# Zero-padded v of the last keys made by GpSimd, preparation at 1.2 items a tile, three splits of nine on VectorE, and three units of weights put together beside attention pairs 3, 6 and 9

## The chip, the cores and the metric

The kernel runs on one core of one Trainium2 chip. The metric is the device time of one execution in microseconds, given as the median of several runs. The engines are named as in the profile: PE is TensorE, PEld its weight loads, DVE is VectorE, ACT is ScalarE, POOL is GpSimd, SP is SyncE, on whose queue all transfers are issued.

## The reference

Three layers in a row, all in float32; the six weight matrices come as float64.

```python
def _attn_ref(q, k, v, tau):                # (4, 8, 576, 64) each
    scores = 1/np.sqrt(64) * np.matmul(q, k.transpose(0, 1, 3, 2))
    thresh = np.max(scores, axis=-1, keepdims=True) - tau
    scores = np.where(scores >= thresh, scores, -1000000000.0)
    scores = scores - np.max(scores, axis=-1, keepdims=True)
    attn = np.exp(scores)
    attn = attn / (np.sum(attn, axis=-1, keepdims=True) + 1e-09)
    return np.matmul(attn, v)
...
x = attn_out.transpose(0, 2, 1, 3).reshape(2304, 512)
g = x @ w_gate                              # (512, 1536)
x = (g / (1 + np.exp(-g)) * (x @ w_val)) @ w_out
return ((x @ w1) * (x @ w2) @ w3) @ w_out2  # d_ff 1024
```

## The kernel before

Every product of large matrices is made of float32r parts: a number is kept as hi plus lo, and hi·hi, hi·lo and lo·hi are added up in PSUM (`mm3`, L835). So every operand must be split into hi and lo first, and much of what the other engines do is such splitting.

**Pairs and tiles.** The attention works on 16 pairs of heads, four to each of the four batches, counted from 0. A pair has nine tiles: four of 128 queries for each of its two heads, and tile 4, which holds the last 64 queries of both. For a tile PE makes the scores into one of two banks S (`mm_scores`, L443); DVE takes the row maximum and brings the scores to SBUF (`el_max`, L482); ACT makes the exponentials (`el_exp`, L491); POOL makes the threshold (`el_thr`, L474); DVE masks and sums (`el_mask`, L501), three tiles behind.

**Two queues of items.** Behind a pair's tile 4 and tile 8 its other work goes into the queue `main`: transposes of the masked tiles through one of four banks T (`it_T`, `it_lq`, `it_kl`, `it_corner`; L328), and the products with v (`it_pv`, L583 and L588). The queue `prep` holds the preparation of the next pair: `it_k`, `it_q` (transposes, hi), `it_k2`, `it_q2` (lo, and transfers that stack hi and lo into L and R) and `it_left` (the last 64 tokens). `it_k` and `it_q` hold a bank T each until `it_k2` and `it_q2` have read it. `some(frac)` runs items by credit: 19.5/9 items of `main` and 0.8 of `prep` a tile. At tile 7 what is left of `prep` is run at once. The instructions written so are then ordered on each engine by a scheduler when the program is built.

**Paths of a split.** The transposed tiles are split out of their bank T by `evac_split` in one of three ways, in the order of the string PATHS: Z: ACT copies hi, PE subtracts it in the bank (L335), ACT copies lo. X: ACT copies hi, DVE subtracts from the bank into lo (L524). Y: ACT copies the bank to SBUF (L535), POOL makes hi (L100) and lo (L103). Before, nine splits in a row are Y Z X Z Y Z X Z Y: three of Y, four of Z, two of X; one copy of path Y in seven goes into a tile of its own, `raw`. In the last pair X and Z take turns.

**v of the last 64 keys.** For the product L588 the v of one head's last 64 keys stands in a tile VLZ of 128 partitions whose other half is zero. `split_left(b)` splits the last v of a batch on POOL into `vls`, once a batch, and `split_v(p)` moves its pair's two parts into VLZ with two transfers on SP (L309).

**Units of weights.** A unit is 128 x 512 numbers of a weight matrix, turned from float64 to hi and lo. `conv_step` starts one unit and ends the one started before: DVE L139, L142, L145, ACT L148, L149, POOL L150 (`conv_bits`), and later DVE L157, ACT L196, and L199 on POOL or DVE by turns. A unit needs a slot of 4 KB a partition. Three slots exist from the start (N_U1), seven more when the last pair begins (N_U2), eight more when its end is near (N_U3).

**The last pair.** When pair 15 begins, `early()` puts seven items into `prep`: three `conv_step` and four `x_prep(0, kk)`, which load the first block of x (the attention's output, through DRAM), add its two halves (POOL L826), multiply by the reciprocal sums (DVE L829) and split it (ACT L817, DVE L818) into four slots; each load takes two slots and gives them back after L829. `begin()` then mixes the first products of the second layer (`glu_step`, L835) with the attention's last items. Every `glu_step` needs its three units put together (`conv_until`).

Of the kernel before, what the change touches and what calls it, by code (L numbers as in the profile page):

```python
# [9 lines left out]
F32 = mybir.dt.float32  # L10
F32R = mybir.dt.float32r
# [12 lines left out]
N_U1, N_U2, N_U3, N_U4 = 3, 7, 8, 24  # L24
N_TMP, N_BIG, N_HB, N_TA = 6, 3, 3, 1

GROUP = 2

PATHS, LAST = "YZXZYZXZY", "XZ"
# [3 lines left out]
def kernel(  # L35
# [171 lines left out]

    def conv_step(n=1):

        old = []  # L210
        while conv_mid and conv_mid[0][2]() and len(old) < n:
            old.append(conv_mid.popleft())
            old[-1][1](conv_value(old[-1][0]))
        new = 0
        while (conv_in or conv_raw) and len(conv_mid) < n:
            conv_fetch()
            raw, *rest = conv_raw.popleft()
            conv_mid.append((conv_bits(raw), *rest))
            new += 1
        conv_fetch()  # L220
        return old or new
# [6 lines left out]
    def attention(actx, early, tail):  # L228
# [8 lines left out]
        ta = lctx.enter_context(tc.tile_pool(name="ta", bufs=N_TA))  # L237
        raw_i, in_tail = [0], []

        def raw_tile():  # L240
            raw_i[0] += 1
            if in_tail or raw_i[0] % (N_TA + N_TMP) >= N_TA:
                return tmp()
            return ta.tile([P, 512], F32, tag="raw", name="raw")

# [7 lines left out]
        VLZ = at.tile([P, 2, 2, 2, D], F32R, name="VLZ")  # L253
        nc.gpsimd.memset(f32(VLZ), 0.0)

# [29 lines left out]
        def split_left(b):  # L285
# [11 lines left out]
            vls = wk.tile([P, HP, 2, D], F32R, tag="vls", name="vls", bufs=2)  # L297
            split_pool(vls[:, :, 0, :], vls[:, :, 1, :], vl)
            lsplit[b] = (qks, vls)

        def split_v(p):
# [4 lines left out]
            vls = lsplit[p // HP][1]  # L306
            for h in range(2):
                r = slice(64 * h, 64 * h + 64)
                nc.sync.dma_start(out=f32(VLZ[r, p % 2, h]), in_=f32(vls[r, p % HP]))  # L309
# [100 lines left out]
        def it_left(p):  # L410
            b, hp = divmod(p, HP)
            L, R = qk_tiles(p)
            qks = lsplit[b][0]
# [96 lines left out]
        def evac_split(hi, lo, bank):  # L510
# [17 lines left out]
            else:  # L528
                raw = raw_tile()
# [43 lines left out]
        def it_pv(p, h, n):  # L573
# [13 lines left out]
            for e in range(2):  # L587
                nc.tensor.matmul(  # L588
                    o, lhsT=VLZ[:, p % 2, h, :, :].rearrange("p a d -> p (a d)"),
# [107 lines left out]
        def some(frac):  # L697
            credit[0] += 19.5 / 9 * frac
            credit[1] += (1.5 if in_tail else 0.8) * frac
# [9 lines left out]
        for n, (p, i) in enumerate(tiles):  # L709
# [25 lines left out]
            if n == NS // 2:  # L735
                conv_fetch()
# [218 lines left out]
    def early():  # L955
        add_slots(ctx.enter_context(tc.tile_pool(name="u2", bufs=1, reuse_waits="tile")), N_U2)
        r = [conv_step] * 3
        for kk in range(KD):
            r.insert(2 * kk + 1, lambda kk=kk: x_prep(0, kk))
        return r  # L960
# [172 lines left out]
```

## Time and profile before

| | |
|---|---|
| median of 3 runs | 1187.19 us (1186.79 to 1188.41) |
| the profiled execution | 1189.26 us, its span 1187.3 us |
| PE busy | 1122.1 us, 95% |
| DVE busy | 733.1 us, 62% |
| ACT busy | 590.3 us, 50% |
| POOL busy | 475.7 us, 40% |
| granted TensorE clock, mean | 0.991 |

The span is the time from the first to the last instruction of the profiled execution; some 2 us lie around it. The attention takes the first 360 us, the second layer ends near 815 us, w3 times w_out2 is made from there to 895 us, and the third layer follows. A busy share over the whole span averages over these stages, so the rows below are taken from single stretches. The clock is given as a share of 2.4 GHz; its two levels are 1.2 and 2.4 GHz.

### The profile page before, as it was taken

What the parts mean: (1) busy time and instruction counts of PE and PEld (TensorE: products, weight loads), DVE (VectorE), ACT (ScalarE), POOL (GpSimd) and SP (SyncE); (2) the same over time, 40 slices, a digit from 0 to 9 for tenths busy, and PEclk for the clock granted to TensorE, in tenths of its full rate; (3) what the DMA queues carried; (4) which work ended last, traced back from release to release, by engine and by line L of the source; (5) the groups of instructions that cost most, each with busy time, mean ns of one, the idle gap of its engine ahead of it and who ended that gap; (6) DMA issues with size and microseconds to landing.
All of it is one profiled execution on the core that took longest, in us unless ns stands there. A gap on an engine that the chain in (4) does not pass through costs nothing.

```text
span 1187.3 us, 16882 instructions
## 1 busy us (share of the span) xinstructions
PE 1122.1 (95%) x6074; PEld 959.8 (81%) x6074; DVE 733.1 (62%) x1272; ACT 590.3 (50%) x1071; POOL 475.7 (40%) x457
## 2 busy tenths in 40 slices
PE   7898998899878999999999999999899999999998
PEld 6788888788766777888888888888787888888886
DVE  7987868778798797656464664567892022432222
ACT  6877878778786456443242432345563231321111
POOL 4575665565663655443232332234241221321110
PEclk9999999999989999999999999999999999999999
DMA  8865756656455743222111120123430010100024
GB/s 197 224 146 141 163 132 142 146 121 142 107 170 167 216 126 100 75 68 71 31 59 36 37 89 8 47 93 103 124 107 18 1 36 1 37 1 1 1 58 102
DMA packets 107891, 108.14 MB, mean 91 GB/s; under 512 B 48800, under 2 KB 82208, under 8 KB 107808
## 3 DMA queue, kind: packets, MB, share of 16 engines
q1 hardware_dynamic: 107808, 107.06, 34.3%
q8 instruction: 48, 0.79, 0.3%
q14 instruction: 35, 0.29, 0.1%
HBM read 68.16 MB, written 14.23 MB: 69 GB/s over the span
## 4 chain that ended last, share of the span: by engine, by line
PE 55%; DVE 5%; DMA 2%; ACT 1%; issue 1%; POOL 0%; POOLq 0%; DVEq 0%; ACTq 0%
PE t_bank L835 36%; PE s_bank L835 19%; DMA raw<-in_moe_w_dram 2%; DVE tmp L157 1%; DVE slot L818 1%; DVE raw L142 1%; DVE tmp L145 1%; DVE tmp L139 0%; DVE slot L911 0%; PE t_bank L908 0%; DVE slot L199 0%; DVE slot L1022 0%; DVE slot L882 0%; DVE slot L1059 0%; ACT raw L148 0%
## 5 line engine op out<-in xcount | busy, mean ns | idle before, releaser
L835 PE MATMUL t_bank<-slot,slot 128*128 128x512 f32 (+1 forms) x2592 | 559.7, 371 | 5.9 <-DVE slot L818 2.4
L835 PEld LDWEIGHTS t_bank<-slot,slot 128*128 128x128 f32 x2592 | 457.0, 189 | 92.8 <-DVE slot L818 3.3
L835 PE MATMUL s_bank<-h,slot 128*128 128x512 f32 (+1 forms) x720 | 161.9, 372 | 3.4 <-ACT slot L884 2.2
L150 POOL TENSOR_TENSOR raw<-raw 128x512 int32<-128x512 int32 x76 | 84.4, 1111 | 182.1 <-ACT raw L149 171.6
L501 DVE SCALAR_TENSOR_TENSOR P<-P,stat,E 128x576 f32<-128x576 f32 x144 | 148.3, 1043 | 5.6 <-POOL stat L474 3.9
L835 PEld LDWEIGHTS s_bank<-h,slot 128*128 128x128 f32 x720 | 126.8, 190 | 27.1 <-ACT slot L884 2.6
L482 DVE TENSOR_SCALAR_CACHE_REDUCE P<-s_bank,neg 128x576 f32<-128x576 f32 x144 | 114.2, 809 | 55.2 <-PE s_bank L443 55.2
L1069 DVE TENSOR_TENSOR tmp<-tmp,t_bank 128x512 f32<-128x512 f32 (+1 forms) x40 | 25.3, 633 | 178.2 <-PE t_bank L835 178.2
L107 POOL TENSOR_TENSOR h<-tmp,h 128x512 fp32r<-128x512 f32 (+1 forms) x60 | 74.4, 1239 | 136.1 <-ACT h L106 136.0
L1073 POOL TENSOR_TENSOR h<-tmp,h 128x512 fp32r<-128x512 f32 (+1 forms) x38 | 45.8, 1205 | 200.5 <-ACT h L1071 200.5
L491 ACT ACTIVATE E<-P,stat 128x576 f32<-128x576 f32 x144 | 116.4, 812 | 9.7 <-DVE P L482 8.8
L443 PE MATMUL s_bank<-R,L 128*128 128x288 f32 x512 | 101.2, 318 | 14.7 <-DVE P L482 5.6
L920 DVE TENSOR_TENSOR tmp<-tmp,t_bank 128x512 f32<-128x512 f32 (+1 forms) x60 | 37.9, 631 | 113.1 <-PE t_bank L835 104.5
L835 PE MATMUL s_bank<-slot,h 128*128 128x512 f32 x432 | 106.6, 391 | 0.9 <-DVE slot L1059 0.8
L328 PE MATMUL t_bank<-ident,P 128*128 128x128 f32 x640 | 90.5, 277 | 14.5 <-DVE AT L524 4.7
L443 PEld LDWEIGHTS s_bank<-R,L 128*128 128x128 f32 x512 | 76.8, 194 | 26.7 <-DVE P L482 15.1
L835 PEld LDWEIGHTS s_bank<-slot,h 128*128 128x128 f32 x432 | 79.9, 188 | 18.3 <-DVE slot L1059 2.1
L882 DVE TENSOR_TENSOR slot<-s_bank,slot 128x1024 f32<-128x1024 f32 (+1 forms) x72 | 82.2, 1146 | 18.5 <-PE s_bank L835 16.5
L328 PEld LDWEIGHTS t_bank<-ident,P 128*128 128x128 f32 x640 | 74.2, 141 | 23.5 <-DVE ATL L524 4.6
L583 PE MATMUL t_bank<-AT,sp 128*128 128x288 f32 x512 | 87.5, 307 | 5.3 <-DVE AT L524 2.4
L157 DVE SCALAR_TENSOR_TENSOR tmp<-tmp,raw 128x512 f32<-128x512 f32 x76 | 72.0, 948 | 30.5 <-POOL raw L150 30.5
L919 ACT ACTIVATE tmp<-t_bank 128x512 f32<-128x512 f32 (+1 forms) x60 | 33.2, 554 | 113.3 <-PE t_bank L835 106.9
(110 smaller groups left out, 1427.9 us busy)
## 6 DMA issues: line engine op xcount, KB each, us to landing
raw<-in_moe_w_dram SPq DMA_DIRECT2D x32, 512.0 KB, 3.8
raw<-in_moe_w_out_dram SPq DMA_DIRECT2D x20, 512.0 KB, 3.5
x_dram<-xs SPq DMA_DIRECT2D x64, 144.0 KB, 2.4
L<-qhi SPq DMA_DIRECT2D x60, 128.0 KB, 2.9
L<-qlo SPq DMA_DIRECT2D x60, 128.0 KB, 2.5
raw<-in_moe_w_gate_dram SPq DMA_DIRECT2D x12, 512.0 KB, 3.7
raw<-in_moe_w_val_dram SPq DMA_DIRECT2D x12, 512.0 KB, 3.8
ld<-in_k_dram SPq DMA_DIRECT2D x16, 256.0 KB, 4.0
```

The costliest lines, as they stand in the source:

```text
L107: nc.gpsimd.tensor_tensor(out=lo, in0=src, in1=f32(hi), op=ALU.subtract)
L150: nc.gpsimd.tensor_tensor(out=a, in0=a, in1=x, op=ALU.subtract)
L157: nc.vector.scalar_tensor_tensor(out=f32(m), in0=f32(m), scalar=2.0 ** 20, in1=f32(a), op0=ALU.add, op1=ALU.mult)
L328: nc.tensor.matmul(bank[:, t * P:(t + 1) * P], lhsT=part, rhs=ident, is_transpose=True, start=(t == 0), stop=(t == len(parts) - 1),)
L443: nc.tensor.matmul(o, lhsT=lhs, rhs=R[:, c:c + HALF], start=(h == hs2[0] and e == 0), stop=(h == hs2[-1] and e == 1),)
L482: nc.vector.tensor_scalar(out=p_tile(p, i).rearrange("p (a c) -> p a c", a=2), in0=sb[:, :, 0:HALF], scalar1=neg, scalar2=None, op0=ALU.mu ...
L491: nc.scalar.activation(out=e, in_=p_tile(p, i), func=ACTF.Exp, scale=-1.0, bias=stats[p // HP][:, 0, c:c + 1],)
L501: nc.vector.scalar_tensor_tensor(out=t, in0=t, scalar=stats[b][:, 1, c:c + 1], in1=e, op0=ALU.is_le, op1=ALU.mult, accum_out=sums[b][:, c: ...
L583: nc.tensor.matmul(o, lhsT=vs[:, 4 * h + c, :, :].rearrange("p a d -> p (a d)"), rhs=AT[h][:, e, c, cs], start=(c == 0 and e == 0), stop=F ...
L835: nc.tensor.matmul(o, lhsT=lhs(a), rhs=rhs(c), start=(first and i == 0), stop=(last and i == 2))
L882: nc.vector.tensor_tensor(out=a, in0=s, in1=a, op=ALU.add)
L1073: (nc.vector if end else nc.gpsimd).tensor_tensor(out=h[:, 1, 0:n], in0=ab[:, 0:n], in1=f32(h[:, 0, 0:n]), op=ALU.subtract)
```

## The change

- VLZ becomes two tiles, one for the even and one for the odd batches, each with all four pairs of a batch. `split_left` splits v right into them, a head's half of the partitions at a time: four POOL operations a batch instead of two, and no `vls` and no transfers.
- `prep` runs 1.2 items a tile instead of 0.8.
- PATHS becomes X Z Y X Z Z Y X Z: three of X, four of Z, two of Y. The extra tile for `raw` goes.
- At tile 4 of pairs 3, 6 and 9 a `conv_step` and a new `conv_end`, which ends a started unit, are put into `prep`. `early()` then holds the four `x_prep` alone.
- Slots: six instead of seven when the last pair begins, nine instead of eight later.

The diff, without its two hunks that only take `ta` and `raw_tile` out:

```diff
-N_U1, N_U2, N_U3, N_U4 = 3, 7, 8, 24
+N_U1, N_U2, N_U3, N_U4 = 3, 6, 9, 24
+EARLY = (3, 6, 9)
-PATHS, LAST = "YZXZYZXZY", "XZ"
+PATHS, LAST = "XZYXZZYXZ", "XZ"
...
+    def conv_end(n=1):
+        old = 0
+        while conv_mid and conv_mid[0][2]() and old < n:
+            bits, done, _ = conv_mid.popleft()
+            done(conv_value(bits))
+            old += 1
+        return old
...
-        VLZ = at.tile([P, 2, 2, 2, D], F32R, name="VLZ")
-        nc.gpsimd.memset(f32(VLZ), 0.0)
+        VLZ = [at.tile([P, HP, 2, 2, D], F32R, name=f"VLZ{n}") for n in range(2)]
+        for t in VLZ:
+            nc.gpsimd.memset(f32(t), 0.0)
...
-            vls = wk.tile([P, HP, 2, D], F32R, tag="vls", name="vls", bufs=2)
-            split_pool(vls[:, :, 0, :], vls[:, :, 1, :], vl)
-            lsplit[b] = (qks, vls)
+            for h in range(2):
+                r = slice(64 * h, 64 * h + 64)
+                split_pool(VLZ[b % 2][r, :, h, 0, :], VLZ[b % 2][r, :, h, 1, :], vl[r])
+            lsplit[b] = qks
...
-            vls = lsplit[p // HP][1]
-            for h in range(2):
-                r = slice(64 * h, 64 * h + 64)
-                nc.sync.dma_start(out=f32(VLZ[r, p % 2, h]), in_=f32(vls[r, p % HP]))
...
-                    o, lhsT=VLZ[:, p % 2, h, :, :].rearrange("p a d -> p (a d)"),
+                    o, lhsT=VLZ[b % 2][:, hp, h, :, :].rearrange("p a d -> p (a d)"),
...
-            credit[1] += (1.5 if in_tail else 0.8) * frac
+            credit[1] += (1.5 if in_tail else 1.2) * frac
...
-            if n == NS // 2:
-                conv_fetch()
+            if i == 4 and p in EARLY:
+                prep.extend([conv_step, conv_end])
...
     def early():
         add_slots(ctx.enter_context(tc.tile_pool(name="u2", bufs=1, reuse_waits="tile")), N_U2)
-        r = [conv_step] * 3
-        for kk in range(KD):
-            r.insert(2 * kk + 1, lambda kk=kk: x_prep(0, kk))
-        return r
+        conv_fetch()
+        return x_items(0)
```

The scheduler makes more of it than these lines tell. The rows below are its order of one engine's instructions; the lines of the changed kernel are numbered some three lower (L479, L498 and L521 are the maximum, the mask and the split of path X; L141 to L159 the steps of a unit on DVE, two higher; L826 and L815 the multiplication and split of x). Over the whole program the counts change so: POOL's two operations of path Y 48 to 32 each, DVE's split of path X 40 to 56, transfers 32 fewer; the numbers of PE's and ACT's instructions stay.

DVE early in the last pair, pair 15 (its P tiles are P_4485 to P_4489), before:

```order
L139 TENSOR_SCALAR tmp<-raw 128x512 x3
L482 TENSOR_SCALAR P_4487,stat<-s_bank,neg 128x576
L142 TENSOR_SCALAR raw<-raw 128x512
L145 SCALAR_TENSOR_TENSOR tmp<-raw,tmp 128x512
L482 TENSOR_SCALAR P_4488,stat<-s_bank,neg 128x576
L829 TENSOR_TENSOR tmp<-tmp,slot_4543 128x512
L142 TENSOR_SCALAR raw<-raw 128x512
L145 SCALAR_TENSOR_TENSOR tmp<-raw,tmp 128x512
L501 SCALAR_TENSOR_TENSOR P_4485,sums<-P_4485,stat,E 128x576
L142 TENSOR_SCALAR raw<-raw 128x512
L145 SCALAR_TENSOR_TENSOR tmp<-raw,tmp 128x512
```

and after (P_4467 to P_4471):

```order
L498 SCALAR_TENSOR_TENSOR P_4468,sums<-P_4468,stat,E 128x576
L479 TENSOR_SCALAR P_4469,stat<-s_bank,neg 128x576
L479 TENSOR_SCALAR P_4470,stat<-s_bank,neg 128x576
L498 SCALAR_TENSOR_TENSOR P_4469,sums<-P_4469,stat,E 128x576
L479 TENSOR_SCALAR P_4471,stat<-s_bank,neg 128x576
L498 SCALAR_TENSOR_TENSOR P_4470,sums<-P_4470,stat,E 128x576
L479 TENSOR_SCALAR P_4467,stat<-s_bank,neg 128x576
L826 TENSOR_TENSOR tmp<-tmp,slot_4502 128x512
L521 TENSOR_TENSOR AT<-t_bank,AT 128x512
L479 TENSOR_SCALAR P_4468,stat<-s_bank,neg 128x576
L498 SCALAR_TENSOR_TENSOR P_4471,sums<-P_4471,stat,E 128x576
```

The steps of the units, L139 to L145 here and L157 and L199 further on, are gone from between the pair's maxima and masks.

DVE at the turn from pair 3 to pair 4, where the reciprocal of the sums of the first batch (`r`) is made, before:

```order
L606 TENSOR_SCALAR r<-sums 128x36
L609 RECIPROCAL r<-r 128x36
L482 TENSOR_SCALAR P_1260,stat<-s_bank,neg 128x576
L482 TENSOR_SCALAR P_1261,stat<-s_bank,neg 128x576
L482 TENSOR_SCALAR P_1262,stat<-s_bank,neg 128x576
L501 SCALAR_TENSOR_TENSOR P_1260,sums<-P_1260,stat,E 128x576
L524 TENSOR_TENSOR AT<-t_bank,AT 128x512
L482 TENSOR_SCALAR P_1263,stat<-s_bank,neg 128x576
```

and after:

```order
L141 TENSOR_SCALAR tmp<-raw 128x512
L603 TENSOR_SCALAR r<-sums 128x36
L144 TENSOR_SCALAR raw<-raw 128x512
L147 SCALAR_TENSOR_TENSOR tmp<-raw,tmp 128x512
L606 RECIPROCAL r<-r 128x36
L479 TENSOR_SCALAR P_1264,stat<-s_bank,neg 128x576
L479 TENSOR_SCALAR P_1265,stat<-s_bank,neg 128x576
L159 SCALAR_TENSOR_TENSOR tmp<-tmp,raw 128x512
L498 SCALAR_TENSOR_TENSOR P_1264,sums<-P_1264,stat,E 128x576
L498 SCALAR_TENSOR_TENSOR P_1265,sums<-P_1265,stat,E 128x576
```

The whole of a unit now stands here among the maxima and masks, but for L201, which POOL has for this one.

PE in the preparation of a later pair (`ld` are k and q as loaded, `khi` and `qhi` their hi parts), before:

```order
L328 MATMUL t_bank<-ident,ld_1570 128x128 x4
L335 MATMUL t_bank<-AT,minus_r 128x512
L328 MATMUL t_bank<-ident,P_1549 128x128
L328 MATMUL t_bank<-ident,P_1550 128x128
L328 MATMUL t_bank<-ident,P_1551 128x128
L328 MATMUL t_bank<-ident,P_1552 128x128
L443 MATMUL s_bank<-R,LZ 128x288 x8
L563 MATMUL t_bank<-ident,P_1553 128x128
L564 MATMUL t_bank<-ident,P_1553 64x128
L443 MATMUL s_bank<-R,L 128x288 x4
L335 MATMUL t_bank<-khi,minus_r 128x512
L328 MATMUL t_bank<-ident,ld_1572 128x128 x4
```

and after:

```order
L325 MATMUL t_bank<-ident,ld_1573 128x128 x4
L325 MATMUL t_bank<-ident,ld_1575 128x128 x4
L440 MATMUL s_bank<-R,LZ 128x288 x8
L440 MATMUL s_bank<-R,L 128x288 x4
L325 MATMUL t_bank<-ident,P_1549 128x128
L325 MATMUL t_bank<-ident,P_1550 128x128
L325 MATMUL t_bank<-ident,P_1551 128x128
L325 MATMUL t_bank<-ident,P_1552 128x128
L332 MATMUL t_bank<-AT,minus_r 128x512
L332 MATMUL t_bank<-khi,minus_r 128x512
L332 MATMUL t_bank<-qhi,minus_r 128x512
```

The transposes of k and q have moved next to each other, and so have the subtractions that free their banks.

## Rows read from the trace of the kernel before

**Rows 1.** The page of the profile, part 1 (busy us, share of the span, instructions).

```profile
PE 1122.1 (95%) x6074; PEld 959.8 (81%) x6074; DVE 733.1 (62%) x1272; ACT 590.3 (50%) x1071; POOL 475.7 (40%) x457
```

**Rows 2.** Stretches: start:end, length, busy PE, PEld, DVE, ACT, POOL (instructions), clock, DMA, GB/s.

```profile
26.50:328.60 302.10, 272.26 (x1954) 247.64 (x1953) 246.20 (x562) 244.67 (x496) 181.69 (x206) 0.99 0.63 147
328.60:359.30 30.70, 22.37 (x138) 19.31 (x137) 30.70 (x56) 25.42 (x47) 19.82 (x16) 0.89 0.60 179
...
475.00:815.00 340.00, 340.00 (x1681) 288.75 (x1680) 194.84 (x264) 124.88 (x203) 113.99 (x97) 1.00 0.19 58
```

**Rows 3.** Waits of PE in pair 15 (us in total, times, longest).

```profile
PE t_bank L328 <- DVE ATL L524: 3.3, 1, 3.3
```

**Rows 4.** DVE's groups of the units in pair 15: xcount | busy us, mean ns | idle.

```profile
L157 DVE SCALAR_TENSOR_TENSOR tmp<-tmp,raw 128x512 f32<-128x512 f32 x3 | 4.2, 1411 | 0.0
...
L145 DVE SCALAR_TENSOR_TENSOR tmp<-raw,tmp 128x512 f32<-128x512 uint16 x3 | 2.4, 816 | 0.0
L142 DVE TENSOR_SCALAR raw<-raw 128x512 int32<-128x512 int32 x3 | 2.4, 812 | 0.0
...
L199 DVE TENSOR_TENSOR slot<-tmp,slot 128x512 fp32r<-128x512 f32 x1 | 1.7, 1749 | 0.0
L139 DVE TENSOR_SCALAR tmp<-raw 128x512 int32<-128x512 int32 x4 | 1.6, 445 | 0.0
```

**Rows 5.** Stretches: pairs 3, 4, 6 and 9 (columns as in rows 2).

```profile
67.30:88.60 21.30, 19.27 (x142) 17.56 (x141) 19.02 (x43) 17.52 (x36) 13.93 (x17) 1.00 0.71 162
88.60:111.10 22.50, 20.70 (x140) 18.75 (x139) 16.66 (x39) 17.32 (x37) 11.07 (x13) 0.92 0.58 135
133.50:154.40 20.90, 19.54 (x143) 17.57 (x142) 15.93 (x39) 17.52 (x37) 13.26 (x16) 1.00 0.63 146
196.90:221.50 24.60, 21.25 (x146) 19.49 (x145) 17.53 (x40) 17.86 (x37) 14.03 (x17) 0.93 0.54 125
```

**Rows 6.** The page, part 5, of DVE's line L157.

```profile
L157 DVE SCALAR_TENSOR_TENSOR tmp<-tmp,raw 128x512 f32<-128x512 f32 x76 | 72.0, 948 | 30.5 <-POOL raw L150 30.5
```

**Rows 7.** Line L524 in pairs 1 to 14 (ns: least, median, most).

```profile
L524 DVE TENSOR_TENSOR AT<-t_bank,AT x28: 675/680/690, 25.9 to 322.2; 128x512 fp32r<-128x512 f32 x28
L524 DVE TENSOR_TENSOR ATL<-t_bank,ATL x3: 679/680/681, 75.5 to 271.4; 128x512 fp32r<-128x512 f32 x3
```

**Rows 8.** Groups of lines in pairs 1 to 14: the mask.

```profile
L501 DVE SCALAR_TENSOR_TENSOR P<-P,stat,E 128x576 f32<-128x576 f32 x129 | 135.2, 1062 | 5.6 <-POOL stat L474 3.9 <-ACT E L491 1.6
```

**Rows 9.** Instructions in order of time: two masks and a subtract of path Y.

```profile
322.79 0.80 DVE L501 SCALAR_TENSOR_TENSOR P<-P,stat,E 128x576 f32<-128x576 f32 x1
...
323.07 1.66 POOL L103 TENSOR_TENSOR AT<-tmp,AT 128x512 fp32r<-128x512 f32 x1
...
323.52 1.83 DVE L501 SCALAR_TENSOR_TENSOR P<-P,stat,E 128x576 f32<-128x576 f32 x1
```

**Rows 10.** Line L103 up to pair 14 on GpSimd (ns: least, median, most).

```profile
L103 POOL TENSOR_TENSOR AT<-tmp,AT x36: 1267/1292/1795, 24.5 to 323.1; 128x512 fp32r<-128x512 f32 x36
...
L103 POOL TENSOR_TENSOR AT<-raw,AT x6: 1272/1291/1794, 62.1 to 297.0; 128x512 fp32r<-128x512 f32 x6
L103 POOL TENSOR_TENSOR ATL<-tmp,ATL x5: 1292/1796/1837, 34.1 to 314.7; 128x512 fp32r<-128x512 f32 x5
```

**Rows 11.** Waits of PE in pairs 1 to 14 (us in total, times, longest).

```profile
PE t_bank L328 <- DVE AT L524: 4.7, 5, 1.1
PE s_bank L443 <- DVE AT L524: 4.2, 2, 2.2
...
PE s_bank L443 <- DMA L<-qlo: 2.1, 4, 1.3
...
PE t_bank L583 <- DVE AT L524: 1.5, 2, 1.1
```

**Rows 12.** The head, in order of time.

```profile
1.54 0.52 POOL L254 MEMSET VLZ<- 128x512 f32 x1
...
4.78 2.50 PE L382 MATMUL t_bank<-ident_r,slot 128*128 128x128 f32 x16 [4.78 <-DVE slot L398]
```

More of the change, by code (lines that the diff above doesn't have):

```diff
@@ L22 @@
 N_THR, N_E = 2, 3
-N_U1, N_U2, N_U3, N_U4 = 3, 7, 8, 24
-N_TMP, N_BIG, N_HB, N_TA = 6, 3, 3, 1
+N_U1, N_U2, N_U3, N_U4 = 3, 6, 9, 24
+N_TMP, N_BIG, N_HB = 6, 3, 3
 GROUP = 2
-PATHS, LAST = "YZXZYZXZY", "XZ"
+EARLY = (3, 6, 9)
+PATHS, LAST = "XZYXZZYXZ", "XZ"
 @with_exitstack
@@ L206, in conv_fetch @@
             conv_raw.append((conv_load(src), *rest))
+    def conv_end(n=1):
[5 more added lines that the diff above has]
+        return old
     def conv_step(n=1):
[L210 to L213, printed above, removed]
+        old = conv_end(n)
         new = 0
@@ L236, in attention @@
         sp = lctx.enter_context(tc.tile_pool(name="sp", bufs=1))
[L237 to L244, printed above, removed]
+        in_tail = []
         ATT = at.tile([P, 2, 2, 4, S], F32R, name="AT")
@@ L412, in it_left @@
             L, R = qk_tiles(p)
-            qks = lsplit[b][0]
+            qks = lsplit[b]
             bank = t_bank()
@@ L528, in evac_split @@
             else:
-                raw = raw_tile()
+                raw = tmp()
                 rv = raw
```

## The prediction

> **What bounds the kernel now.** I read three views, in this order. First the busy shares: TensorE (PE) is at work for 1122.1 us, 95% of the span [rows 1], so at most 65 us in all can be won, and only where PE waits. Then the table of stretches, to find where that is. From 475 to 815 us PE is busy without a break [rows 2]; nothing that the other engines do there shows in the time. Ahead of it, pairs 1 to 14 of the attention hold 29.8 us of idle PE (302.10 less 272.26) and pair 15 holds 8.3 (30.70 less 22.37) [rows 2].
>
> I cut the stretches at the start of each pair's first row maximum (L482, every ninth of 144). Pairs 1 to 14 take 21.6 us each on average, with PE idle 2.1 us of it and VectorE (DVE) 4.0 us (302.10 less 246.20, by 14). They are PE's. Pair 15 takes 30.7 us, and DVE is busy for all 30.70 of them. That pair alone is DVE's. Third, the waits of PE: one of pair 15's lasts 3.3 us and ends with a split on DVE [rows 3]. The clock shows a second loss there: the granted clock is 0.89 in that pair, so PE ran at the lower of its two levels for part of it, and 0.11 of 30.7 us, 3.4 us, went that way.
>
> **The units of weights.** Before, three units are put together in pair 15. Their DVE work there is 4.2 + 2.4 + 2.4 + 1.7 us and three of the four L139 of 0.445 us, 1.3 us: 12.0 us together [rows 4]. The change takes all of it out, as the order of DVE shows. What pair 15 then takes I work out twice. By PE: 22.37 less the 3.4 us lost to the clock is 19.0, and with the 2.1 us of waits of a usual pair 21.1, so 9.6 us less. By DVE: 30.7 less 12.0 is 18.7, and with the usual 4.0 us of idle 22.7, so 8.0 us less. I take **-9**. The bounds are -12.0, all of the DVE work, and -2, if something else holds the pair (first rival).
>
> The same 12.0 us of DVE work now stand beside pairs 3, 6 and 9, where DVE was idle 2.3, 5.0 and 7.1 us [rows 5]: 14.4 us of cover, and more in the pairs behind them, since the order puts the last steps at the turn to the next pair. But a step that stands on DVE in front of a maximum delays PE, whose two score banks it frees; and the last step of a unit on DVE's queue, L157, waits there for GpSimd's L150 with all that stands behind it: 0.4 us a unit in the mean (30.5 us over 76) [rows 6]. I take **+3**, a quarter of the work. Bounds: 0, and +12.0 with the cover gone. ScalarE and GpSimd get their shares of the three units too; both are idle for more of these pairs than PE is [rows 5].
>
> **The splits.** By the order sixteen splits go from path Y (ScalarE copies the bank out, GpSimd makes hi and lo) to path X (ScalarE makes hi, DVE makes lo from the bank). ScalarE's work stays one copy each. DVE gets 16 x 0.680 = 10.9 us [rows 7]. Against that stands what GpSimd's subtract does to DVE's mask (L501). It takes 0.80 us undisturbed, 1.062 in the mean over 129 [rows 8]: some 33.8 us of excess. In one look at both engines the mask that starts at 323.52 lasts 1.83 us beside a subtract of path Y, and the one ahead of it 0.80 [rows 9]. There are 36 + 6 + 5 such subtracts up to pair 14 [rows 10]; if they make all of the excess, each costs 0.72 us, and sixteen fewer give 11.5 us back. So DVE's total changes by between -0.6 and +10.9 us; I take 0, since the look shows the two together.
>
> The Trainium skill (SBUF — State Buffer, "Who interferes with whom") says that a DVE instruction with two SBUF inputs contends with a GpSimd one that reads SBUF, and one with at most one SBUF input does not. By that rule X's subtract from PSUM is never slowed and the swap is free, as I took it; that it lasts between 0.675 and 0.690 us [rows 7] agrees. By the same rule a unit's own steps with two inputs in SBUF are slowed beside path Y, and the cost of the units would lie above its quarter.
>
> What X costs is the bank. Y frees its bank (four are shared) after ScalarE's copy; X only after DVE has come round to it. PE waited 4.7 + 4.2 + 1.5 = 10.4 us for such splits in pairs 1 to 14 [rows 11], over 31 of them [rows 7]: 0.34 us each. Sixteen more at that price are +5.4; with masks no longer stretched in front of them, less. I take **+2**; bounds 0 and +5.4, and beyond in the last rival but one.
>
> **Preparation at 1.2 items a tile.** Its five items are spread over 4.2 tiles instead of 6.3. k's and q's transposes then stand next to each other on PE, as the order shows, and the two banks that they hold until their lo is made are held for 1.7 tiles instead of 2.5. The stacked L lands sooner too: PE waited 2.1 us for L<-qlo [rows 11], and in pair 4 the granted clock is 0.92 [rows 5], which is 1.8 us of its 22.5. I take **-2**, the wait; bounds -3.9, both, and +2.1, if the crowded items make PE wait once more as long as in a usual pair.
>
> **v of the last keys.** 32 transfers leave SyncE's queue; PE felt that queue only in the 2.1 us just counted. GpSimd gets eight operations more; even at the 1.3 us of a subtract of twice their size [rows 10] that is 10 us, less than the sixteen subtracts of path Y that it loses, 21 us. So nothing, since GpSimd idles 120 us in pairs 1 to 14 [rows 2]; with that cover gone, masks would wait for the thresholds on its queue. The zero fill grows from 0.52 us to four times the elements, 2.1, and if it stands ahead of the identity it delays the first transposes, which start at 4.78 us behind DVE's splits [rows 12]: **+0.5**; bounds 0 and +1.6.
>
> **Sum:** -9 + 3 + 2 - 2 + 0.5 = -5.5 us. The profiled execution took 1189.26 us around its span of 1187.3, 2.07 above the median of 1187.19; against the median the forecast is 1181.7, said as **1181.5**.
>
> **Rivals.**
> *The first block of x holds pair 15.* The four items x_prep stay there, and with six slots where there were ten each load waits for the multiplication before it. If the first products of the next layer start no earlier for that, some 2 of the 9 us remain: 1181.7 + 7 = 1188.7, no change that a measurement can tell. For it: all four stand in that pair on DVE and GpSimd one behind the other. Against: DVE, which multiplies, had no idle moment in pair 15 [rows 2], so its queue, and not the load, was the likelier delay.
>
> *The attention gains as well.* If the units are hidden whole and X costs nothing, the sum is -9 + 0 + 0 - 3.9 + 0.5 = -12.4; the second low clock in the pairs (0.93 in pair 9, 1.7 us) [rows 5] goes too if its wait goes: -14.1, 1173.1. For it: 14.4 us of idle DVE. Against: PE is at 90% in these pairs, and its waits are short and many.
>
> *DVE gets too much.* If the units' 12.0 us are not hidden at all, 1190.7; with half of them hidden, 1184.7. The Trainium skill's page Perfetto Trace Analysis ("Optimizing Scalar/DVE Operations") advises to take work off DVE where it is saturated; the change puts more on it. In pairs 1 to 14 DVE is busy 81% of the time [rows 2], which speaks against this rival.
>
> *Banks wait for X, and the kernel is slower.* The place is PE's next transpose or score, behind a split that stands on DVE behind two masks and, in three pairs, a unit. The price is 47 splits times the mean wait. It decides from a mean of 0.43 us: 20.2 us are 9.8 more than the 10.4 of now, where I allowed 2, and end 2.3 above the median. At 0.55 us it is 25.9, and the time 1195. For it: 0.34 is not far from 0.43. Against: the masks ahead get shorter.
>
> *The change doesn't do what it says:* a scheduler orders each engine, and could put the units elsewhere. The order shows them where they should be; the time would be one of the above.
>
> **How the numbers follow.** My case 0.47 (its own range 1178 to 1185); attention gains as well 0.20; x holds pair 15 0.09; too much for DVE 0.11, half of it slower; banks wait for X 0.13. No change means within 0.2%, 2.4 us, about what a measurement of this kernel can tell. My case and the second are faster but for a small tail: 0.66. No change: 0.17. Slower: 0.17. The range reaches from 1173, the second case, to 1191, the third; about 1 in 10 lies under it and 1 in 10 above.
>
> **What would show it.** Pair 15: 21 to 23 us instead of 30.7, DVE with idle time in it, no L139 to L157 in it, no low clock. Pairs 3, 6 and 9: longer by 1 us each, no more. The mask's mean down from 1.062 to about 0.97 us. PE's waits for DVE's splits at 12 to 13 us, and none for L<-qlo. It is wrong if pair 15 stays above 26 us, if PE's idle time in pairs 1 to 14 grows by over 6 us, or if the masks are no faster with sixteen subtracts fewer.

## The result, and the profile after

| | median of runs | range | profiled execution, span |
|---|---|---|---|
| before | 1186.79 us (7) | 1185.05 to 1190.63 | 1189.26, 1187.3 us |
| the change | 1201.93 us (7) | 1195.28 to 1205.30 | 1198.62, 1196.8 us |

The change is slower: ratio 1.0112, 95% interval 1.0082 to 1.0141, 13 us by the ratio and 15 by the medians. The forecast of 1181.5 us was wrong in its sign, and its range of 1173 to 1191 does not hold the time. The profiled execution of the change lies 3.3 us below its median, so the two traces show 9.5 us of difference in the span, not all of it.

The page after, part 1; it answers to [rows 1]:

```profile
PE 1124.2 (94%) x6074; PEld 961.4 (80%) x6074; DVE 725.3 (61%) x1288; ACT 590.3 (49%) x1071; POOL 436.6 (36%) x434
```

PE has the same work. DVE is 7.8 us below its 733.1, and POOL 39.1 us below its 475.7: neither is what got longer. Below are stretches of the change (start:end, length, busy PE, PEld, DVE, ACT, POOL, clock, DMA, GB/s); the first two and the last answer to [rows 2]. The fifth reaches from PE's first transposes to its last product with v. Behind them stand two stretches of before, that same one and the one from pair 15 to that product:

```profile
29.10:335.70 306.60, 268.70 (x1914) 244.16 (x1913) 251.60 (x589) 247.56 (x498) 148.27 (x180) 0.98 0.61 140
335.70:352.30 16.60, 14.85 (x108) 13.26 (x107) 14.56 (x34) 13.01 (x26) 9.32 (x10) 1.00 0.47 130
352.30:386.00 33.70, 27.71 (x170) 23.44 (x171) 21.36 (x38) 21.32 (x42) 9.98 (x8) 1.00 0.59 170
386.00:1196.80 810.80, 792.77 (x3775) 663.87 (x3773) 417.64 (x577) 290.79 (x476) 253.30 (x210) 0.99 0.21 62
5.80:386.00 380.20, 331.37 (x2302) 297.46 (x2303) 305.34 (x701) 298.24 (x595) 180.20 (x215) 0.99 0.63 147
475.00:815.00 340.00, 340.00 (x1677) 288.56 (x1676) 193.71 (x260) 128.03 (x206) 116.14 (x99) 1.00 0.18 57
```

```profile
4.80:380.60 375.80, 332.36 (x2302) 298.22 (x2303) 312.68 (x694) 299.86 (x598) 220.62 (x240) 0.98 0.64 155
328.60:380.60 52.00, 40.38 (x241) 34.00 (x240) 50.35 (x91) 40.28 (x74) 28.46 (x23) 0.93 0.59 176
```

Pairs 1 to 14 (first row) take 306.6 us instead of 302.1, and PE is idle for 37.9 of them instead of 29.8. Pair 15 (second row) fell from 30.7 to 16.6 us, more than I forecast, but most of that is no gain: items of `main` were left over, and between the last maximum and the last product with v (third row) PE had 27.7 us of work to do. From the start of pair 15 to that product it is 50.3 us (16.6 + 33.7) instead of 52.0. What counts is PE's lost time up to that product: idle time plus what the lower clock cost. By the granted clock of the trace it is 43.4 + 6.8 = 50.2 us before, and 48.8 + 5.1 = 53.9 us after, with pair 15 and what follows it down by 7.3 us and pairs 1 to 14 up by 9.8. The last product with v starts at 386.0 us instead of 380.6. From there to the end it is 810.8 us instead of 806.7, of which the clock takes 6.9 instead of 3.8; from 475 to 815 us PE is busy throughout, as before.

The waits of PE in pairs 1 to 14 of the change (us in total, times, longest), beside [rows 11]:

```profile
PE s_bank L440 <- DMA L<-qlo: 6.2, 6, 1.9
...
PE t_bank L325 <- DVE ATL L564: 3.1, 4, 1.0
...
PE t_bank L325 <- DVE AT L521: 2.1, 3, 1.0
...
PE t_bank L418 <- POOL stat L471: 2.0, 1, 2.0
PE t_bank L325 <- ACT klo L342: 1.9, 3, 0.8
PE t_bank L418 <- DVE ATL L564: 1.7, 2, 1.1
```

Waits for path X's split (L521) are small here, where L524 cost 10.4 us before. New are the waits of L418, the transposes of `it_left`; and L325, P's and the preparation's transposes, waits for banks that other items hold (klo, the corner ATL L564). Over all rows, PE waits 17.1 us for a bank T, where it waited 11.6 before; and in front of scores 12.4 us for L and R that landed late or with no releaser shown, where it was 2.3. The experiments have to tell which of the two is the loss. DVE in the same stretch, which answers to [rows 4, 8], and the split X, which answers to [rows 7]:

```profile
L498 DVE SCALAR_TENSOR_TENSOR P<-P,stat,E 128x576 f32<-128x576 f32 x129 | 120.7, 951 | 11.4 <-POOL stat L471 7.4 <-ACT E L488 1.8 <-ACT xs L592 1.3
...
L147 DVE SCALAR_TENSOR_TENSOR tmp<-raw,tmp 128x512 f32<-128x512 uint16 x3 | 3.1, 1038 | 0.0
...
L144 DVE TENSOR_SCALAR raw<-raw 128x512 int32<-128x512 int32 x3 | 2.6, 859 | 0.0
L159 DVE SCALAR_TENSOR_TENSOR tmp<-tmp,raw 128x512 f32<-128x512 f32 x3 | 2.1, 684 | 0.0
L141 DVE TENSOR_SCALAR tmp<-raw 128x512 int32<-128x512 int32 x3 | 1.3, 418 | 0.0
L201 DVE TENSOR_TENSOR slot<-tmp,slot 128x512 fp32r<-128x512 f32 x1 | 1.1, 1129 | 0.0
```

```profile
L521 DVE TENSOR_TENSOR AT<-t_bank,AT x42: 673/684/693, 28.4 to 333.8; 128x512 fp32r<-128x512 f32 x42
L521 DVE TENSOR_TENSOR ATL<-t_bank,ATL x4: 679/682/683, 102.1 to 309.2; 128x512 fp32r<-128x512 f32 x4
```

The masks are shorter (0.951 instead of 1.062 us), and the three units cost DVE 3.1 + 2.6 + 2.1 + 1.3 + 1.1 = 10.2 us, less than the 12.0 they took in pair 15.

### The profile page after: what moved, and what is told of

The parts are those of the page before. It is cut to its first block, busy times and chain, and to the rows that moved or that the text cites. A ratio compares the mean times of both kernels' runs of the same rounds, so it can differ in the third digit from the quotient of the medians.

```text
span 1196.8 us, 16816 instructions
## 1 busy us (share of the span) xinstructions
PE 1124.2 (94%) x6074; PEld 961.4 (80%) x6074; DVE 725.3 (61%) x1288; ACT 590.3 (49%) x1071; POOL 436.6 (36%) x434
## 4 chain that ended last, share of the span: by engine, by line
PE 65%; DVE 16%; DMA 7%; issue 4%; ACT 4%; SPq 2%; POOL 2%; ACTq 0%; DVEq 0%; POOLq 0%
PE t_bank L832 36%; PE s_bank L832 18%; PE t_bank L580 4%; DVE P L498 4%; DVE P L479 4%; PE s_bank L440 3%; DMA raw<-in_moe_w_dram 2%; PE t_bank L325 2%; DVE slot L815 1%; DMA L<-qlo 1%; DVE tmp L159 1%; SPq L792 1%; DMA slot<-r_dram 1%; DVE tmp L147 1%; PE t_bank L585 1%
## 5 line engine op out<-in xcount | busy, mean ns | idle before, releaser
L498 DVE SCALAR_TENSOR_TENSOR P<-P,stat,E 128x576 f32<-128x576 f32 x144 | 135.2, 953 | 13.3 <-POOL stat L471 8.4
L479 DVE TENSOR_SCALAR_CACHE_REDUCE P<-s_bank,neg 128x576 f32<-128x576 f32 x144 | 114.0, 810 | 41.8 <-PE s_bank L440 39.8
L440 PE MATMUL s_bank<-R,L 128*128 128x288 f32 x512 | 97.8, 314 | 21.4 <-DVE P L479 6.4
L325 PE MATMUL t_bank<-ident,P 128*128 128x128 f32 x640 | 92.3, 278 | 12.2 <-DVE ATL L564 3.1
L159 DVE SCALAR_TENSOR_TENSOR tmp<-tmp,raw 128x512 f32<-128x512 f32 x76 | 68.6, 903 | 39.2 <-POOL raw L152 39.2
L325 PEld LDWEIGHTS t_bank<-ident,P 128*128 128x128 f32 x640 | 74.4, 141 | 21.5 <-ACT klo L342 3.0
L150 ACT ACTIVATE raw<-raw,ebias 128x512 int32<-128x512 int32 x76 | 57.9, 763 | 64.5 <-DVE tmp L147 47.9
L580 PE MATMUL t_bank<-AT,sp 128*128 128x288 f32 x512 | 86.7, 306 | 1.8 <-DVE AT L521 1.6
```

What stands on the lines that cost most here:

```text
L150: nc.scalar.activation(out=a, in_=x, func=ACTF.Relu, scale=8.0, bias=ebias[:, 0:1])
L159: nc.vector.scalar_tensor_tensor(out=f32(m), in0=f32(m), scalar=2.0 ** 20, in1=f32(a), op0=ALU.add, op1=ALU.mult)
L325: nc.tensor.matmul(bank[:, t * P:(t + 1) * P], lhsT=part, rhs=ident, is_transpose=True, start=(t == 0), stop=(t == len(parts) - 1),)
L440: nc.tensor.matmul(o, lhsT=lhs, rhs=R[:, c:c + HALF], start=(h == hs2[0] and e == 0), stop=(h == hs2[-1] and e == 1),)
L479: nc.vector.tensor_scalar(out=p_tile(p, i).rearrange("p (a c) -> p a c", a=2), in0=sb[:, :, 0:HALF], scalar1=neg, scalar2=None, op0=ALU.mu ...
L498: nc.vector.scalar_tensor_tensor(out=t, in0=t, scalar=stats[b][:, 1, c:c + 1], in1=e, op0=ALU.is_le, op1=ALU.mult, accum_out=sums[b][:, c: ...
```

## The experiments

The table has all runs; "left" is the item `it_left`, and where a row names a kernel of this table, the edit stands on that one. Each ratio is to the kernel before, run beside it on the same chip. "Units alone" has the slots of the change; "VLZ by POOL alone" has them too, and lacks the extra tile for `raw`.

| label | kernel | median us (runs) | ratio to before, 95% |
|---|---|---|---|
| u_prep | change, 0.8 again | 1186.0 (10) | 0.9978, 0.996 to 0.9996 |
| u_units | change, units in pair 15 again | 1205.9 (4) | 1.0149, 1.0128 to 1.017 |
| u_paths | change, old PATHS | 1199.3 (4) | 1.0096, 1.0073 to 1.0119 |
| u_vlz | change, old VLZ with transfers | 1195.9 (7) | 1.0064, 1.0041 to 1.0086 |
| a_prep | before, 1.2 alone | 1205.3 (4) | 1.013, 1.0098 to 1.0162 |
| a_units | before, units alone | 1182.1 (4) | 0.9938, 0.9915 to 0.9961 |
| a_paths | before, new PATHS alone | 1187.3 (10) | 0.999, 0.9969 to 1.001 |
| a_vlz | before, VLZ by POOL alone | 1188.1 (10) | 0.9987, 0.9975 to 0.9999 |
| m_order | change, k, k2, q, q2, left | 1190.6 (10) | 1.0027, 1.0006 to 1.0048 |
| m_left | change, left in tile 7 | 1185.0 (10) | 0.9976, 0.9955 to 0.9996 |
| m_left5 | change, left in tile 5 | 1187.3 (10) | 0.999, 0.9977 to 1.0004 |
| a_prep_left | a_prep, left in tile 7 | 1190.6 (10) | 1.0004, 0.9986 to 1.0021 |
| b_units_left | a_units, 1.2, left in tile 7 | 1189.2 (10) | 1.0002, 0.9979 to 1.0026 |
| l_t3 | u_prep, left in tile 3 | 1190.1 (10) | 1.0015, 0.9996 to 1.0035 |
| l_early | u_prep, left in tile 4 | 1201.8 (4) | 1.0105, 1.0069 to 1.0141 |
| l_t5 | u_prep, left in tile 5 | 1180.5 (4) | 0.9924, 0.99 to 0.9947 |
| u_prep_paths | u_prep, old PATHS | 1180.9 (4) | 0.9917, 0.9895 to 0.9939 |
| b_t5_paths | l_t5, old PATHS | 1183.3 (6) | 0.9956, 0.994 to 0.9973 |

### Which part it is

Each part was undone in the change; u_vlz turns the diff's hunks of VLZ and `vls` round, its transfers included, and keeps the tiles and slots of the change:

```diff
u_prep   -            credit[1] += (1.5 if in_tail else 1.2) * frac
         +            credit[1] += (1.5 if in_tail else 0.8) * frac
u_units  -            if i == 4 and p in EARLY:
         -                prep.extend([conv_step, conv_end])
         +            if n == NS // 2:
         +                conv_fetch()
...
         -        conv_fetch()
         -        return x_items(0)
         +        r = [conv_step] * 3
         +        for kk in range(KD):
         +            r.insert(2 * kk + 1, lambda kk=kk: x_prep(0, kk))
         +        return r
u_paths  -PATHS, LAST = "XZYXZZYXZ", "XZ"
         +PATHS, LAST = "YZXZYZXZY", "XZ"
```

> The changed kernel with 0.8 items of preparation a tile instead of 1.2. In the trace of the change, PE waits 12.4 us in pairs 1 to 14 in front of scores for late stacked L and R or with no releaser shown (2.3 us before). Theory P (the faster preparation lets scores run ahead and lays the transfers of k and q on one heap): those waits fall to under 4 us and the time to 1190 us or less, ratio to before 1.002 or less. Rivals, theory U (the units beside pairs 3, 6 and 9) and theory X (three splits of nine on DVE): the time stays within 3 us of the change, about 1202 us, ratio 1.01.

> The changed kernel with the three units put together in pair 15 as before (the slots stay six and nine). Theory U: pairs 1 to 14 get 6 us or more shorter, but pair 15 grows back from 16.6 to about 28 us: the time comes to 1195 us or less. Theories P and X: pairs 1 to 14 stay as long as in the change, 306 us, and pair 15's gain is lost: 1206 to 1212 us, ratio 1.017 to 1.022.

> The changed kernel with the string of paths of before (three Y, two X of nine). Theory X: PE's and DVE's waits around banks and splits in pairs 1 to 14 fall and the time is 1193 us or less. Theories P and U: the masks get slower again (mean from 0.95 to 1.06 us), 13 us more on DVE, and the time stays at 1200 us or goes up to 1206.

> The changed kernel with v of the last keys moved by transfers as before (32 transfers on SyncE's queue, and no extra operations of GpSimd). All of theories P, U and X: no change over 3 us against the change, 1199 to 1205 us. If SyncE's queue is what holds PE up in the change, 1205 to 1210, since 32 transfers of about 0.5 us join it.

Only u_prep gives the loss back, 15.9 us of it. Its time is the one of theory P, but not its mechanism: the waits for L and R were to fall under 4 us, and L<-qlo alone takes 6.7 (its row stands further down). Undoing the paths brings 2.6 us, less than the two intervals can tell apart. Undoing v brings 6, more than any of the theories allowed, with intervals that just touch; no run here says why. Undoing the units makes it worse: they are the part that wins. Then two parts alone in the kernel before, the same lines as above with the signs turned:

> The kernel before with 1.2 items of preparation a tile and nothing else. Theory P (the faster preparation alone costs what the change lost): pairs 1 to 14 grow by 8 us or more and the time to 1197 to 1204 us, ratio 1.007 to 1.013. Rival (the preparation is harmful only together with the units beside the pairs or the third split on DVE): within 3 us of before, ratio 0.998 to 1.003.

> The kernel before with the three units beside pairs 3, 6 and 9, slots six and nine, preparation at 0.8, the old paths and the old transfers of v. If the units are what gains (my 9 us less in pair 15 against 3 more beside the pairs): 1180 to 1185 us, ratio 0.993 to 0.998, pair 15 at 21 to 23 us. If the gain of the last experiment came from the splits instead: 1187 to 1191 us.

Preparation at 1.2 alone costs 16 us, the units alone win 7. The stretches of a_units show that win where I had put it, pairs 1 to 14 and then from pair 15 to the last product with v (columns as above):

```profile
26.60:331.50 304.90, 272.16 (x1954) 246.63 (x1954) 255.88 (x575) 250.05 (x505) 187.48 (x211) 0.99 0.64 148
331.50:374.10 42.60, 38.39 (x240) 33.36 (x239) 37.59 (x72) 32.01 (x61) 18.70 (x17) 0.96 0.58 176
```

In the second, PE's idle time is 4.2 us (42.60 less 38.39) where before it is 11.6, and 1.7 us go to the clock instead of 3.4: 9.1 us less lost. In the first, PE loses 36.1 us instead of 33.2. So -9 and +3.

### What it is in the preparation

At 0.8 items a tile `it_left`, the last of the five, comes in tile 6, at 1.2 in tile 4. Two edits of the change keep 1.2 for the other items:

```diff
m_order -            return [lambda f=f: f(p) for f in (it_k, it_q, it_k2, it_q2, it_left)]
        +            return [lambda f=f: f(p) for f in (it_k, it_k2, it_q, it_q2, it_left)]
m_left  -            return [lambda f=f: f(p) for f in (it_k, it_q, it_k2, it_q2, it_left)]
        +            return [lambda f=f: f(p) for f in (it_k, it_q, it_k2, it_q2)]
...
                     while prep:
                         run_item(prep.popleft())
        +            if p + 1 < NP:
        +                run_item(lambda: it_left(p + 1))
```

> The changed kernel, preparation still at 1.2, but its items in the order k, lo of k, q, lo of q, left, so that one bank T is held at a time instead of two. Theory B (two of the four banks held together, right where the pair's other transposes start, is how 1.2 costs time): 1186 to 1193 us, ratio under 1.004. Rival S (1.2 costs by putting PE's and ScalarE's work of the preparation too early, whatever its order): 1198 to 1204 us, ratio 1.009 to 1.013.

> The changed kernel, preparation at 1.2, but its last item, the transposes of the last 64 tokens, held back to tile 7 as 0.8 items a tile had it. PE waited 3.9 us in front of these transposes in the change and not at all with 0.8. Theory L (this item, in front of PE's queue while the banks are full, is the cost): 1186 to 1193 us. Theories B and S: it gives back at most those 3.9 us, 1197 to 1204 us.

Either takes most of the loss away: m_left 17 us, m_order, in which k's lo is made before q takes a bank, 11. m_order leaves `it_left` where the change has it, so at 1.2 that place costs its full price only with k's and q's transposes side by side; and m_left has these side by side in 14 of the 15 preparations, so they alone cost nothing that shows. Below are m_left up to its last product with v, and from 28 to 335 us, which holds its pairs 1 to 14, all waits of PE for a bank T but one of 0.2 us, beside those for a transfer:

```profile
5.80:373.60 367.80, 330.52 (x2301) 297.20 (x2302) 297.98 (x700) 296.46 (x594) 179.39 (x215) 0.99 0.65 152
```

```profile
PE s_bank L440 <- DMA L<-qlo: 10.6, 14, 3.5
PE t_bank L580 <- DVE AT L521: 2.0, 2, 1.8
PE t_bank L325 <- DVE AT L521: 1.2, 2, 0.9
...
PE t_bank L325 <- ACT klo L342: 0.5, 2, 0.2
PE t_bank L332 <- ACT AT L511: 0.5, 2, 0.2
```

Late transfers are not it: m_left is fast with 10.6 us of waits for them on PE, as many as the change has (9.8 with a transfer as releaser). The waits for banks T are what goes: 4.4 us instead of 17.1, none of them at L418. PE is idle 37.3 us up to the last product instead of 48.8; the clock takes 5.1 us in both.

The counter-test puts `it_left` alone into tile 4, at the slow rate, and the edit of m_left (in a_prep_left) takes it out of there in the kernel before at the fast rate. Of l_early, which like m_left has four items in `prep_items`:

```diff
             some(0.4)
+            if i == 4 and p + 1 < NP:
+                run_item(lambda: it_left(p + 1))
             es[n] = el_exp(p, i)
```

> The change with preparation back at 0.8 (1186.0 us measured), but left's item run in tile 4 of a pair instead of in tile 6 or 7; the other four items stay where 0.8 puts them. Theory A (left's item is what hurts: in tile 4 its transposes stand on PE among those of P, when the four banks are asked for by P's transposes and held by k and q): 1194 to 1203 us, with PE waiting 2 us or more for left's bank and more than 6 us for those of P. Theory B (the rate as such hurts, five items in fewer tiles, whichever they are): unchanged, 1183 to 1189 us.

> The kernel before with preparation at 1.2 (1205.3 us measured), but left's item held back to tile 7. Theory A (left's item in tile 4): back to 1184 to 1192 us, no wait of PE for left's bank. Theory B (the rate as such): stays above 1198 us. A value between would mean that left's place and the closer order of k and q share the loss.

l_early has the whole loss, 1201.8 against 1186.0 us, and a_prep_left returns 15 us of a_prep's 1205.3. So the theory that the rate as such hurts (B of these two texts) falls twice. The stretch up to the last product with v, and waits of PE in pairs 1 to 14, of u_prep:

```profile
5.70:369.40 363.70, 326.17 (x2302) 294.24 (x2303) 295.66 (x701) 296.90 (x595) 185.36 (x215) 0.99 0.65 155
```

```profile
PE s_bank L440 <- DMA L<-qlo: 6.7, 7, 1.6
...
PE t_bank L332 <- ACT AT L511: 1.8, 4, 0.7
```

and of l_early, with two short stretches that the next paragraph is about:

```profile
5.70:389.10 383.40, 338.10 (x2302) 304.62 (x2303) 305.35 (x701) 296.95 (x595) 185.68 (x215) 0.96 0.61 146
149.90:153.80 3.90, 1.71 (x10) 1.00 (x9) 3.90 (x8) 3.90 (x10) 3.61 (x4) 1.00 1.08 249
153.80:157.20 3.40, 2.82 (x12) 2.85 (x13) 3.40 (x7) 1.64 (x3) 1.44 (x2) 0.50 0.41 86
```

```profile
PE s_bank L440 <- DMA L<-qlo: 10.9, 7, 2.4
PE t_bank L332 <- ACT AT L511: 6.0, 10, 1.0
...
PE t_bank L418 <- POOL AT L105: 1.1, 1, 1.1
...
PE t_bank L418 <- DVE AT L521: 1.0, 2, 0.7
...
PE t_bank L418 <- ACT qlo L342: 0.9, 1, 0.9
PE t_bank L418 <- ACT AT L515: 0.6, 1, 0.6
```

The stretch grows by 19.7 us: PE is idle 45.3 us instead of 37.5, and the clock, 0.96 instead of 0.99, takes 15.4 instead of 3.4 by the trace. That is more than the 15.8 us between the medians, since the profiled execution of u_prep, 1179.6 us, is the fastest of its ten. L418 now waits 3.6 us, where u_prep has no such wait, and the subtractions L332 wait for ACT 6.0 us instead of 1.8; all waits for banks T are 16.9 us instead of 7.1. L<-qlo rises too, from 6.7 to 10.9 us, but m_left bears that much without the loss. One place in l_early, in order of time (start, us):

```profile
149.38 0.60 PE L325 MATMUL t_bank<-ident,P 128*128 128x128 f32 x4
...
150.16 0.68 ACT L342 ACTIVATE qlo<-t_bank 128x512 fp32r<-128x512 f32 x1
...
150.88 0.53 PE L418 MATMUL t_bank<-ident_r,qkls 128*128 128x128 f32 x4 [0.91 <-ACT qlo L342]
...
151.36 0.66 PE L325 MATMUL t_bank<-ident,P 128*128 128x128 f32 x4
...
151.79 0.67 ACT L511 CAST AT<-t_bank 128x512 fp32r<-128x512 f32 x1
...
152.25 0.49 ACT L310 ACTIVATE LZ<-t_bank 128x256 fp32r<-128x256 f32 x1
...
152.51 0.50 PE L332 MATMUL t_bank<-AT,minus_r 128*128 128x512 f32 x1 [0.49 <-ACT AT L511]
152.53 0.49 ACT L310 ACTIVATE R<-t_bank 128x128 fp32r<-128x128 f32 x2
```

PE ends P's transposes at 149.98 and stands still until 150.88: the next instruction on its queue is L418, and its bank is free only when ACT has read q's lo out of it (150.16 to 150.84). P's next transposes, which wait behind it, start at 151.36, then the subtraction L332 waits for ACT, which comes to its copy (L511) only at 151.79, with no pause since 149.69. The copies of `it_left` stand behind that one here, so they are not what L332 waits for; what makes these waits longer over the whole of l_early is open. L418's own bank is not read out before 153 us, by three copies (the first at 152.25). In 149.90:153.80 PE shows 1.71 us of work, and in the 3.4 us behind it (153.80:157.20) the granted clock is 0.50: 2.2 us of idle PE are followed here by 1.7 us lost to the clock.

The Trainium skill (Perfetto Trace Analysis, "Optimization Strategy") says that a gap that repeats on the engine that should be saturated can mean too little PSUM for the next tile: the waits of L418 agree, but the banks were four in every kernel here, and only the order in which PE asks for them changed.

Where exactly the item stands was tried in two more tiles, in both by the `i ==` of l_early:

> The change with preparation back at 0.8 and left's item run in tile 3 of a pair (in tile 6 or 7: 1186.0 us; in tile 4: 1201.8 us). Theory A1 (it hurts where the transposes of P's second half ask for banks, which the queue of main items brings in tiles 3 to 5): 1195 to 1205 us. Theory A2 (it hurts because it stands ahead of q's and k's low halves, so a third bank is taken while both are held): more than in tile 4, 1202 to 1212 us, since both low halves are still to be made there.

> As l_t3, but left's item in tile 5, where the last of P's transposes of a pair are issued and q's low half comes in the same tile. Theory A1: between the two, 1189 to 1197 us. Theory A2: 1184 to 1190 us, as both low halves are made or nearly so. If it is the tile 4 alone that hurts, 1186 us.

> The change itself, all four other items at 1.2 as it has them, with left's item in tile 5 of a pair, where its transposes stand on PE behind the last of P's (1201.9 us with left's item where 1.2 puts it, in tile 4; 1185.0 in tile 7). Theory A (the place behind P's last transposes is what counts): 1179 to 1187 us. Rival (at the fast rate the four others fill the banks, and left's item has to wait for tile 7): above 1190 us.

Tile 5 is the best of the four, 1180.5 us, below all three ranges set for it, and up to the last product with v PE is idle for 34.4 us only (361.60 less 327.21):

```profile
5.70:367.30 361.60, 327.21 (x2301) 295.25 (x2302) 299.74 (x696) 297.19 (x593) 184.86 (x215) 0.99 0.65 154
```

PE's order shows where tile 5 differs: rows of l_early and then of l_t5, in the preparation of the same pair (each P0 begins one item of P's transposes, `qkls` is `it_left`, L580 is the product with v):

```
L325 MATMUL t_bank_1392<-ident_71,P0_959 128x128
...
L418 MATMUL t_bank_1401<-ident_r_72,qkls_918 128x128 x4
...
L325 MATMUL t_bank_1418<-ident_71,P0_959 128x128
...
L580 MATMUL t_bank_1437<-AT_108,sp2_1221 128x288 x8
```

```
L325 MATMUL t_bank_1410<-ident_71,P0_959 128x128
...
L580 MATMUL t_bank_1442<-AT_108,sp2_1221 128x288 x8
...
L418 MATMUL t_bank_1456<-ident_r_72,qkls_918 128x128 x4
L580 MATMUL t_bank_1473<-AT_108,sp2_1221 128x288 x8
```

In tile 4 `it_left` asks for a bank ahead of the last of P's transposes, in tile 5 behind them, between products with v. So in all the orders: ahead of one to three items of P's transposes, in 14 of the 15 preparations, it stands in the change, u_units, u_paths, u_vlz, a_prep, l_early, m_order and l_t3, which took 1190.1 to 1205.9 us; behind all of them in the eleven other kernels of the table and in the one before, 1180.5 to 1190.6. PE's waits for banks T in pairs 1 to 14 part the same way, one trace of each kernel: 13.4 to 18.8 us in the first group, 2.5 to 12.0 in the second. m_left5 shows the place at 1.2, with 14.7 us of the loss back, though at 1187.3 us it is 7 above l_t5. The size is not settled by the place, nor by these waits: m_order (16.3 us of them) and l_t3 (17.5) are the mild ones of the first group, no slower than the slowest of the second. l_t3 is a miss of A1 and A2 both, 4 us above u_prep and 10 above l_t5 where 9 to 26 above u_prep were expected. In most preparations of l_t3, m_order and l_early alike k's subtraction stands ahead of q's transposes, and l_early has the whole loss. Why tile 3 is cheaper than tile 4 is open.

### The other terms

> The kernel before with the new order of splits alone (three more on VectorE, fewer by GpSimd's subtract). Forecast term: +2 us with bounds 0 and +5.4, so 1189 to 1194 us, against a median before of 1189.0. If GpSimd's subtract beside the masks costs as much as the split itself: 1187 to 1190 us.

> The kernel before with v of the last keys padded by GpSimd itself instead of by 32 transfers, and with the tile that this frees (seven buffers of the raw splits become six, the slots of the units 6 and 9 instead of 7 and 8). Forecast term: 0 us, 1187 to 1191 us. If the 32 transfers held anything up that the attention waits for: 1182 to 1186 us; if the sixteen narrower splits, or six buffers, hold GpSimd or the splits up: above 1192 us.

Both alone are within a measurement of nothing. On u_prep and l_t5 going back to the old paths gave opposite signs:

> The change with preparation back at 0.8 and with the old order of splits: what is left of the change is the units beside pairs 3, 6, 9 and v of the last keys by GpSimd. If moving the three splits to VectorE is free (GpSimd's subtract slows the masks instead): within 3 us of the 1186.0 measured with the new order. If the splits on VectorE cost what the ratio of the units alone suggests (1182.05 us): 1180 to 1183 us.

> The change with preparation at 0.8, left's item in tile 5, and the old order of the splits. If the new order costs about 5 us wherever left's item stands: 1174 to 1178 us. If what it cost at the slow rate (1186.0 against 1180.9) was left's item in tile 6 or 7 beside it: 1179 to 1183 us, as l_t5.

It is 5 us faster in one and 3 slower in the other, where the two intervals still touch. So no price of the order of the splits holds in all the kernels; that it depends on where the other items stand is likely, but not shown. Last, the version with the units and 1.2 but `it_left` held back:

> The kernel before with the units beside pairs 3, 6, 9 (1182.05 us measured alone), and with preparation at 1.2 with left's item held back to tile 7. Theory A: no loss against the units alone, 1178 to 1185 us; if the four other items at 1.2 still cost something by themselves: 1186 to 1192 us.

It is 7 us slower than a_units: the four other items at 1.2 are not free there, although m_left is no slower than u_prep. That is not settled. Three versions beat both kernels by most: u_prep_paths, l_t5 and a_units, 0.6 to 0.8% below before. None is told from the others by these intervals.

## Why the prediction was wrong

**The step that failed is "Preparation at 1.2 items a tile": -2 us, bounds -3.9 and +2.1.** It measured about +16 us, alone (a_prep) and by undoing it (u_prep). I looked at how long k and q hold their banks, and at L<-qlo. I did not look at the fifth item: at 1.2 it leaves the products with v and arrives ahead of P's transposes, which take their banks from the same four. PE's order shows L418 there in 14 of 15 preparations. Its bank then waits for another item's copy or split, and on PE's one queue all stands still behind it. My upper bound, one usual pair's wait of 2.1 us, counted a single event. The change waits 12.7 us more for banks T than m_left (17.1 against 4.4), whose edit moves this item alone and which is 17 us faster. L<-qlo did not go either, it rose from 2.1 to 6.2 us. Why a place ahead of P's transposes is cheap in m_order and l_t3 stays open.

**Units: right.** -9 + 3 = -6 against 6.8 us measured in the median, and both terms show in a_units' lost time, -9.1 and +2.9. But pair 15 at "21 to 23 us" was a poor test: at 16.6 it looked better than forecast while most of its work was only moved behind it.

**Splits: the masks right, DVE's total and the waits not.** The masks did what I forecast: over all 144 their mean is 0.92 to 0.97 us in the traces of all kernels with the new order, 0.98 to 1.05 with the old. In pairs 1 to 14 their excess over 0.80 us fell from 33.8 to 129 x 0.151 = 19.5 us, 14.3 less, and sixteen splits of X brought 10.9. I gave DVE's total 0, between -0.6 and +10.9; the page shows -7.8, and a_paths, the order alone, -7.5 (725.6). But this total is no clean measure: in a_prep, which gives DVE the same instructions as before, it is 727.5. By the Trainium skill (SBUF — State Buffer, "Who interferes with whom") a DVE instruction with at most one SBUF input, outside the 2-port modes, does not contend with GpSimd; L521 at 673 to 693 ns agrees. The +2 for the banks was not seen: alone the new order is at 0.999, 0.9969 to 1.001.

**v and the head: right within bounds, alone.** v alone is at 0.9987, 0.9975 to 0.9999; in the change undoing it gave 6 us back, which this term has no place for. PE's first transposes start at 5.8 us instead of 4.78: +1.0, where I took 0.5 and bounded by 1.6.

**The rivals.** "Banks wait for X" had the sign right, with 1195 us, and it is banks T that PE waits for; but not for X: its splits hold PE for 3.0 us (L325 2.1 us, the rest in two smaller rows), less than before. "DVE gets too much" falls with a_units, where the units cost 2.9 us in pairs 1 to 14. "The first block of x" and "the attention gains as well" are not borne out. My sign of failure, PE's idle time in pairs 1 to 14 up by over 6 us, was met with 8.1; it pointed at the right place.

The parts alone sum to +0.45%, the change to +1.12%. The 8 us between are the parts' effect on each other, if they are real: the intervals of these five ratios, taken together, leave some 6 us open. No single run here assigns them.

## What to carry to other kernels

When a change raises a rate, ask for each item that the rate moves where it will stand in the engine's order, and who asks for the same buffers there; the last item of the queue moves farthest. Price it not by how long it holds its buffer but by what stands behind it while it waits for one. And when a stage gets shorter, count the work of the bounding engine that it hands on before calling it a win.

## Not expected of the hardware

In one pair of traces the clock took more than the waits did. Up to the last product with v l_early has 7.8 us more of idle PE than u_prep (45.3 less 37.5), and 12.0 us more lost to stretches at 0.50, that is 1.2 GHz (15.4 less 3.4); the place above shows one of them behind its waits. It is not always so: a_prep has 10.7 us more of idle PE than a_prep_left and 5.1 us more of the low clock, and the change 11.5 us more of idle PE than m_left and no more of the low clock. These are single executions, and one kernel's executions lie farther apart than the terms that were to be told: the change's from 1195.3 to 1205.3 us.
